# A planned attention-and-MLP kernel on one core: batch 0's query denominators in two groups, and its order searched anew

## The chip, the core and the metric

One Trainium2 chip, one of its cores. The time is the device time of one execution in microseconds; runs of one kernel are summed up by their median. Engines are named as in the profile: PE (TensorE), DVE (VectorE), ACT (ScalarE), POOL (GpSimd) and SP (SyncE, which here only issues transfers).

## What is computed

Linear attention with second-degree features, then an MLP on the result, float32 in and out:

```
# q, k, v: (4 batches, 4 heads, 1088 tokens, 32); S1, S2: (8, 32)
a = S1 @ x;  b = S2 @ x                          # per token and head, x is q or k
phi(x) = outer(a, b).reshape(64)
kv = sum over tokens of outer(phi(k), v)         # (64, 32) per batch and head
z  = sum over tokens of phi(k)
num = phi(q) @ kv
den = phi(q) @ z + 1e-6
x = num / den                                    # 4352 tokens, 128 wide (4 heads x 32)
h = x @ w_in                                     # 128 -> 2048
g = h if h >= 1 else 0 if h <= -1 else (h + 1)**2 / 4
out = g @ w_out                                  # 2048 -> 128
```

The weights and S come as float64 and are turned into float32 on the chip.

## The kernel before

**Work and tiles.** The MLP is cut into 9 chunks of 512 tokens (the last has 256) and 16 blocks of 128 hidden features: 144 units (`unit`, L824). A unit multiplies up (L838: three matmuls into a PSUM bank, since x and w_in are each held as a high and a low part), computes g (ACT Relu at L849 and Square at L851, DVE max and min at L854), splits g into a high and a low part (L860, L862 or L854 for the high part, L866 for the low part) and multiplies down into its chunk's sum (L880 twice, L885 once). `KINDS` says for each of the first 48 units which engine makes the high part: c on ACT, q on POOL, v on DVE; p makes the high part on ACT and the low part on DVE; w does not split g and multiplies down with one full float32 matmul (L890, which the trace shows as two records). The low part of c, q and v is made on POOL.

**Attention.** For each batch `keys` (L514) projects k (`abk`, L529), turns the result (`kab`, L535), forms the products phi(k) (`kp`, L553, on POOL where `KP_POOL` names the group, else on DVE) and sums kv (L589) and z (L560, then masked into `zm` at L568 and turned back at L573). `queries` (L616) does the rest. For batch 0 (the loop at L671) the 9 tiles of 128 tokens go in four groups of 2, 2, 3 and 2 tiles. For each group PE projects q (`abq`, L681), ACT copies the first factor out of PSUM (`as`, L689, with the second factor too where POOL is to multiply), DVE multiplies it with the projection on z (`terms`, L692), sums (`den`, L696), inverts (L698) and scales the first factor (`ap`, L701); DVE or, where `QP_POOL` names the group, POOL forms the products (`qp`, L707). PE turns the products (`tp`, L718), they are copied to `qt`, and PE multiplies them with kv (`nd`, L736); the result is split into `x_hi` and `x_lo` (L748). Chunk 0 needs groups 0 and 1, chunk 1 needs the others. The batches 1 to 3 use other code in `queries`, in groups of 3 tiles.

**Weights.** The eight pieces of w_in and w_out (`raw_i`, `raw_o`) are loaded and turned into float32 and into high and low parts (`from_double`, L416): an absolute value on ACT (L435), a clamp on POOL (L441), three integer steps on DVE (L444, L448, L452), the high part on ACT (L469), the low part on POOL, or on DVE where `IN_BANK` keeps the piece in PSUM (L471). Three raw buffers are shared by the eight pieces.

**Order.** Nothing is ordered by hand. Every step gets an engine, a cost and a due time (the constants at L22 to L62), and `Plan.run` (L147) lays the steps out on the five engines in a simulated order: at each moment an engine takes the ready step with the lowest due time for which buffers are free. The program is then issued in that order, so that each engine works through a fixed list and waits where an operand is late. Until the first units, PE's gaps are filled with idle matmuls (`warm`, L354). A down multiplication is due `AFTER` units after its up multiplication. [...]

Loads of batch 0 are split over the queues of SP and ACT; all others go through SP in the planned order.

Of the kernel before, what the change touches and what calls it, by code (L numbers as in the profile page):

```python
# [50 lines left out]
O0 = 0.8
KEYS = {1: (-39.7, -26.1), 2: (-27.9, -34.86), 3: (-37.22, -24.46)}
QEND = ((5.72, -6.14, -2.87), (7.51, 13.24, 4.11), (-9.22, -3.62, -6.11))
QLONG = (26.38, 22.3, 41.07)
FQ = ((-9.85, 4.5), (-11.89, 5.96), (-6.01, 0.82), (-7.59, 9.43))
FK = (-16.26, 9.99)
FKV = 6.85
WI = 5.68
WO = 2.37
# [270 lines left out]
def tile_kernel(ctx: ExitStack, tc: tile.TileContext, qT, kT, v, S, w_in, w_out, outT):  # L330
# [164 lines left out]
    QPART = [0, 0, 1, 1]  # L495
# [120 lines left out]
    def queries(b, kvb, dues):  # L616
# [3 lines left out]
        if not front:  # L620
# [29 lines left out]
            for gi, grp in enumerate(QGRP[b]):  # L650
                d = dues[gi]
                n = len(grp)
                g = slice(grp[0] * H, (grp[-1] + 1) * H)
                pool = (b, gi) in QP_POOL
                eng = nc.gpsimd if pool else nc.vector
                scaled = (lambda g=g: of(ap)[:, g]) if pool else (lambda g=g: kept()[:, g])
                tok = ap.part(gi) if pool else abq[0].part(("ap", gi))
                plan.add(d(0.3), "DVE", dve(n * HR), lambda scaled=scaled, g=g, n=n: nc.vector.tensor_tensor(
                    out=scaled(), in0=flat(0)[:, g], in1=rec()[:, g].broadcast_to([P, n * H, R]), op=ALU.mult),
                    r=[*both, abq[0].part("r")], w=[tok])  # L660
                qp = Buf("qp", f"qp{b}_{gi}", [P, 3, H * F])
# [6 lines left out]
                plan.add(d(0.5), "DVE", turned32(n * H * F), lambda qp=qp, grp=grp, n=n: nc.vector.transpose(  # L668
                    out=of(qt)[:, grp[0] : grp[-1] + 1].rearrange("p t f -> p (t f)"),
                    in_=of(qp)[:, :n].rearrange("p t f -> p (t f)")), r=[qp], w=[qt.part(gi)])  # L670
        for gi, grp in enumerate(QGRP[b] if front else ()):  # L671
# [4 lines left out]
            abc = bank(f"abq{b}_{gi}", tags[0])

            def project(abc=abc, grp=grp):
                for i, t in enumerate(grp):
                    for k, c in enumerate((slice(0, F), slice(F, 2 * F))):  # L680
                        nc.tensor.matmul(of(abc)[c, i * 96 : (i + 1) * 96], lhsT=of(qb)[:, t, c],  # L681
                                         rhs=proj[:, k:][:, :H, : 3 * R], start=True, stop=True)
# [4 lines left out]
            f = 2 if pool else 1
            a = Buf("as", f"as{b}_{gi}", [P, 2, 3 * H, R])
            plan.add(d(0.1), "ACT", act(m * R * f), lambda a=a, view=view, m=m, f=f: nc.scalar.copy(  # L689
                of(a)[:, :f, :m].rearrange("p f m i -> p m f i"), view()[:, :, :f]), r=[abc], w=[a])  # L690
            ti = (4 * b + gi) % 2
            plan.add(d(0.15), "DVE", dve(m * R), lambda a=a, view=view, m=m, ti=ti: nc.vector.tensor_tensor(  # L692
                out=terms[ti][:, :m, :R], in0=of(a)[:, 0, :m], in1=view()[:, :, 2], op=ALU.mult),
                r=[abc, a], w=[("terms", ti)])
            den = Buf("den", f"den{b}_{gi}", [P, 4 * H, 1])
            plan.add(d(0.2), "DVE", dve(m * 9), lambda den=den, m=m, ti=ti: nc.vector.tensor_reduce(  # L696
                out=of(den)[:, :m], in_=terms[ti][:, :m], axis=AX.X, op=ALU.add), r=[("terms", ti)], w=[den])
            plan.add(d(0.25), "DVE", 0.2, lambda den=den, m=m: nc.vector.reciprocal(  # L698
                out=of(den)[:, :m], in_=of(den)[:, :m]), r=[], w=[den])
            ap = Buf("ap", f"ap{b}_{gi}", [P, 3 * H, R])  # L700
            plan.add(d(0.3), "DVE", dve(m * R), lambda den=den, ap=ap, view=view, m=m: nc.vector.tensor_tensor(  # L701
                out=of(ap)[:, :m], in0=view()[:, :, 0], in1=of(den)[:, :m].broadcast_to([P, m, R]), op=ALU.mult),
                r=[abc, den], w=[ap])
# [309 lines left out]
```

## Time and profile before

| | |
|---|---|
| median of 3 runs | 228.28 us (228.09 to 228.99) |
| the profiled execution | 228.78 us |
| its span, first to last instruction | 226.8 us |
| PE busy in the span | 222.3 us (98%) |
| DVE busy | 207.4 us (91%) |
| ACT busy | 193.0 us (85%) |
| POOL busy | 191.7 us (85%) |
| granted TensorE clock | 1.000 of full speed in all slices |

The span is the distance from the first to the last instruction; the rest of the execution's time, 2.0 us, lies around it. Busy times are sums over an engine's instructions; a matmul's end is modelled, so consecutive matmuls overlap in the records and their pace is read from their starts. Engines work in the order of the program; what an instruction waited for is inferred from semaphores.

### The profile page before, as it was taken

The numbers are of one execution on the slowest core, as the hardware profiler recorded it, in microseconds if no ns is written. First come the engines' busy times: TensorE is split into PE (matmuls) and PEld (weight loads), VectorE is DVE, ScalarE is ACT, GpSimd is POOL, SyncE is SP. The second block draws the span as 40 slices with busy tenths as digits, with TensorE's granted clock in tenths as the row PEclk, the third lists the DMA queues.
The fourth block names the chain that finished last, engine by engine and source line by source line (L and its number), as shares of the span: only waits on it lengthen the run. The fifth ranks groups of instructions, "written<-read, shape, count | busy, mean of one in ns | idle before, by whom it ended". The sixth has DMA issues, their size and how long they took to land.

```text
span 226.8 us, 4962 instructions
## 1 busy us (share of the span) xinstructions
PE 222.3 (98%) x1737; PEld 171.3 (76%) x1739; DVE 207.4 (91%) x399; ACT 193.0 (85%) x385; POOL 191.7 (85%) x180
## 2 busy tenths in 40 slices
PE   8999999999999999999999999999999999999994
PEld 2568766778767788887576888888778888898894
DVE  3699989999988899899999999999968999998992
ACT  3279999999986989999586799898739999898993
POOL 5579799999995965999849699999966999999950
PEclk9999999999999999999999999999999999999999
DMA  6993450960001010001000100010000100100001
GB/s 176 411 349 131 135 197 10 353 253 0 0 3 46 8 46 1 0 0 46 3 3 0 49 1 0 1 48 3 0 0 0 49 0 1 46 4 0 0 0 69
DMA packets 4775, 13.86 MB, mean 61 GB/s; under 512 B 528, under 2 KB 912, under 8 KB 4752
## 3 DMA queue, kind: packets, MB, share of 16 engines
q1 hardware_dynamic: 4320, 12.91, 15.9%
q10 hardware_dynamic: 432, 0.66, 0.8%
q8 instruction: 13, 0.21, 0.4%
q14 instruction: 10, 0.08, 0.1%
HBM read 11.34 MB, written 2.23 MB: 60 GB/s over the span
## 4 chain that ended last, share of the span: by engine, by line
PE 95%; DMA 2%; DVE 1%; issue 0%; ACT 0%; POOL 0%; POOLq 0%
PE h L838 42%; PE acc L880 27%; PE acc L885 13%; PE acc L890 2%; DMA k<-in_kT 2%; PE nd L762 2%; PE kv L589 2%; PE abk L529 2%; PE warm L354 1%; PE tp L718 1%; PE abq L635 1%; PE nd L736 1%; PE z L573 1%; PE z L560 0%; PE kv L609 0%
## 5 line engine op out<-in xcount | busy, mean ns | idle before, releaser
L866 POOL TENSOR_TENSOR g_lo<-g,g_hi 128x512 fp32r<-128x512 f32 (+1 forms) x123 | 149.5, 1249 | 17.1 <-DVE g_hi L854 6.8
L849 ACT ACTIVATE s<-h 128x512 f32<-128x512 f32 (+1 forms) x144 | 80.7, 581 | 11.6 <-PE h L838 8.1
L851 ACT ACTIVATE s<-s 128x512 f32<-128x512 f32 (+1 forms) x144 | 86.5, 622 | 2.6
L854 DVE SCALAR_TENSOR_TENSOR g<-h,s 128x512 f32<-128x512 f32 (+1 forms) x123 | 79.7, 651 | 6.4 <-ACT s L851 4.9
L854 DVE SCALAR_TENSOR_TENSOR g_hi<-h,s 128x512 fp32r<-128x512 f32 (+1 forms) x97 | 62.1, 643 | 0.9 <-ACT s L851 0.6
L838 PE MATMUL h<-x_hi,wi_hi 128*128 128x512 f32 (+1 forms) x144 | 56.0, 389 | 0.0
L838 PE MATMUL h<-x_hi,wi_lo 128*128 128x512 f32 (+1 forms) x144 | 54.5, 378 | 0.0
L838 PE MATMUL h<-x_lo,wi_hi 128*128 128x512 f32 (+1 forms) x144 | 54.4, 378 | 0.0
L885 PE MATMUL acc<-g_lo,wo_hi 128*128 128x512 f32 (+1 forms) x138 | 52.8, 384 | 0.0
L880 PE MATMUL acc<-g_hi,wo_hi 128*128 128x512 f32 (+1 forms) x138 | 52.5, 381 | 0.0
L880 PE MATMUL acc<-g_hi,wo_lo 128*128 128x512 f32 (+1 forms) x138 | 52.1, 378 | 0.0
L838 PEld LDWEIGHTS h<-x_hi,wi_hi 128*128 128x128 f32 x144 | 27.1, 188 | 8.0 <-DVE g L854 1.0
L885 PEld LDWEIGHTS acc<-g_lo,wo_hi 128*128 128x128 f32 x138 | 25.9, 188 | 6.8 <-issue 1.2
L838 PEld LDWEIGHTS h<-x_hi,wi_lo 128*128 128x128 f32 x144 | 27.1, 188 | 5.2
L838 PEld LDWEIGHTS h<-x_lo,wi_hi 128*128 128x128 f32 x144 | 27.1, 188 | 4.9 <-issue 0.2
L880 PEld LDWEIGHTS acc<-g_hi,wo_hi 128*128 128x128 f32 x138 | 26.0, 188 | 5.9 <-issue 1.4
L880 PEld LDWEIGHTS acc<-g_hi,wo_lo 128*128 128x128 f32 x138 | 26.0, 188 | 4.6
L553 POOL TENSOR_TENSOR kp<-kab 128x768 f32<-128x768 f32 (+2 forms) x5 | 9.7, 1963 | 1.1 <-DVE kab L535 1.1
L663 POOL TENSOR_TENSOR qp<-ap,qab 128x768 f32<-128x768 f32 x7 | 10.7, 1522 | 0.0
L860 ACT CAST g_hi<-g 128x512 fp32r<-128x512 f32 x16 | 10.0, 633 | 0.6 <-DVE g L854 0.6
L866 DVE TENSOR_TENSOR g_lo<-h,g_hi 128x512 fp32r<-128x512 f32 (+1 forms) x15 | 8.7, 609 | 0.9 <-ACT g_hi L860 0.7
L354 PE MATMUL warm<-const-bfloat16-1.0 128*128 128x512 bf16 x24 | 8.3, 474 | 1.2 <-PEq L1001 0.8
(108 smaller groups left out, 195.6 us busy)
## 6 DMA issues: line engine op xcount, KB each, us to landing
raw_i<-in_w_in SPq DMA_DIRECT2D x4, 512.0 KB, 4.9
raw_o<-in_w_out SPq DMA_DIRECT2D x4, 512.0 KB, 5.2
outT<-o SPq DMA_DIRECT2D x8, 256.0 KB, 2.1
k<-in_kT SPq DMA_DIRECT2D x3, 576.0 KB, 7.7
q<-in_qT SPq DMA_DIRECT2D x3, 576.0 KB, 6.1
v<-in_v SPq DMA_DIRECT2D x3, 576.0 KB, 6.2
k<-in_kT SPq DMA_DIRECT2D x1, 448.0 KB, 4.7
v<-in_v SPq DMA_DIRECT2D x1, 320.0 KB, 6.7
```

What stands on the lines that cost most here:

```text
L354: plan = Plan(rings, lambda n: nc.tensor.matmul(of(warm)[:, :n], lhsT=ones[:, :P], rhs=ones[:, :n], start=True, stop=True), WARM)
L529: nc.tensor.matmul(of(abs_[k])[c, : NTL * D].rearrange("p (t f) -> p t f", f=D), lhsT=s_pair[rows, k * D : (k + 1) * D], rhs=of(kb)[rows, ...
L553: eng.tensor_tensor(out=of(kp)[:, grp[0] : grp[-1] + 1].rearrange("p t (h i j) -> p (t h) i j", h=H, i=R), in0=x[0].unsqueeze(3).broadcast ...
L663: lambda qp=qp, n=n, g=g, eng=eng, scaled=scaled: eng.tensor_tensor(out=of(qp)[:, :n].rearrange("p t (h i j) -> p (t h) i j", h=H, i=R), i ...
L838: nc.tensor.matmul(t[:, cols], lhsT=w[:, fj], rhs=x[:, xs], start=first, stop=last)
L849: plan.add(u, "ACT", act(n2), lambda: nc.scalar.activation(of(s)[:, :n2], of(h)[:, :n2], AF.Relu, bias=0.5, scale=0.5), r=[h], w=[s])
L851: plan.add(u, "ACT", act(n2, False), lambda: nc.scalar.activation(of(s)[:, :n2], of(s)[:, :n2], AF.Square), w=[s])
L854: nc.vector.scalar_tensor_tensor(out=of(out)[:, :n2], in0=of(h)[:, :n2], scalar=1.0, in1=of(s)[:, :n2], op0=ALU.max, op1=ALU.min)
L860: plan.add(u, "ACT", act(n2, False), lambda: nc.scalar.copy(of(g_hi)[:, :n2], of(g)[:, :n2]), r=[g], w=[g_hi])
L866: plan.add(u, "DVE" if late else "POOL", dve(n2) if late else pool_t(n2), lambda: eng.tensor_tensor(out=of(g_lo)[:, :n2], in0=of(g)[:, :n2 ...
L880: nc.tensor.matmul(of(acc)[:, into], lhsT=w[:, fj], rhs=of(g_hi)[:, cols], start=first and i == 0 and w is wo_hi, stop=False)
L885: nc.tensor.matmul(of(acc)[:, into], lhsT=wo_hi[:, fj], rhs=of(g_lo)[:, cols], start=False, stop=last and i == m - 1)
```

## The change

Batch 0's first factors, denominators and scaled factors are made in two groups: one of 4 tiles (the former groups 0 and 1) and one of 5 tiles (2 and 3), each with one projection bank, one copy, one `terms`, `den`, reciprocal and `ap`. The products, turns and everything after them stay in four groups; where POOL multiplies, ACT copies that group's second factor apart. With it, all constants of the order are new, among them the engine that splits each of the first units, which pieces' low parts go to DVE, and which products go to POOL.

```diff
-FILL = -62.42
-KINDS = 'wqcqwcwqcwqcqwvcpcpcpvqqwcpqvvpcvcvqccpcvppcccpq'
+FILL = -20.67
+KINDS = 'wwqccqvpwcwpcqqpqccpvpvqcqwcpcvqqpqqqpvpqqqpccqc'
-IN_BANK = ('i2', 'i3', 'o3')
+IN_BANK = ('i0', 'i2', 'i3', 'o0', 'o2', 'o3')
-AFTER = 6.29
+AFTER = 5.4
-KP_POOL = ((0, 1), (0, 2), (1, 0), (1, 1), (2, 0))
+KP_POOL = ((0, 0), (0, 1), (0, 2), (1, 0), (1, 1), (2, 0), (3, 0))
-QP_POOL = ((0, 3), (1, 0), (1, 1), (1, 2), (2, 0), (2, 2), (3, 1), (3, 2))
+QP_POOL = ((0, 1), (0, 3), (1, 0), (1, 1), (1, 2), (2, 0), (2, 1), (3, 0), (3, 2))
...
+        for ci, pair in enumerate(((0, 1), (2, 3)) if front else ()):
+            d = dues[pair[0]]
+            tiles = [t for gi in pair for t in QGRP[b][gi]]
...
+            plan.add(d(0.0), "PE", n * ABQ, project, r=[qb.part(ci), "proj"], w=[abc]).kind(1, 8 * n)
...
+            plan.add(d(0.1), "ACT", act(m * R), lambda a=a, view=view, m=m: nc.scalar.copy(
+                of(a)[:, 0, :m], view()[:, :, 0]), r=[abc], w=[a])
...
         for gi, grp in enumerate(QGRP[b] if front else ()):
...
-            plan.add(d(0.0), "PE", n * ABQ, project, r=[qb.part(QPART[gi]), "proj"], w=[abc]).kind(1, 8 * n)
...
+            abc, view, a, ap, g = chains[gi]
             pool = (b, gi) in QP_POOL
...
+            if pool:
+                plan.add(d(0.2), "ACT", act(m * R), lambda a=a, view=view, g=g: nc.scalar.copy(
+                    of(a)[:, 1, g], view()[:, g, 1]), r=[abc], w=[a.part(gi)])
```

The names in the lists below carry the batch or group first: `abq_1` is the projection of group 1, `mi` and `mo` are a piece of w_in or w_out on its way, `mago` its absolute value, `hci` and `hco` its clamp. The line numbers of the changed kernel are those of before up to L491, then mostly one less in `keys` and eight more behind the query code.

First ACT, from the projection of batch 0's queries on. Before:

```order
L689 COPY as_1_230<-abq_1_219 128x64
L689 COPY as_0_240<-abq_0_225 128x64
L469 CAST wi_hi<-magi_170 128x512
L689 COPY as_3_258<-abq_3_232 128x8x2x8
L689 COPY as_2_278<-abq_2_243 128x96
L435 ACTIVATE mago_280<-raw_o_126 128x512
```

and changed:

```order
L469 CAST wi_hi<-mi_189 128x512
L435 ACTIVATE mago_231<-raw_o_126 128x512
L710 COPY as_0_248<-abq_0_220 128x64
L687 COPY as_0_248<-abq_0_220 128x128
L710 COPY as_1_268<-abq_1_235 128x64
L687 COPY as_1_268<-abq_1_235 128x160
```

The weight steps `wi_hi` and `mago` now stand ahead of the first `as`, and `mago` reads a transferred piece.

Then DVE, at the denominators. Before:

```order
L692 TENSOR_TENSOR terms_85<-as_1_230,abq_1_219 128x8x8
L696 TENSOR_REDUCE den_1_250<-terms_85 128x8
L692 TENSOR_TENSOR terms_83<-as_0_240,abq_0_225 128x8x8
L698 RECIPROCAL den_1_250<-den_1_250 128x8
L696 TENSOR_REDUCE den_0_256<-terms_83 128x8
L701 TENSOR_TENSOR ap_1_272<-abq_1_219,den_1_250 128x64
L698 RECIPROCAL den_0_256<-den_0_256 128x8
L707 TENSOR_TENSOR qp_1_282<-ap_1_272,abq_1_219 128x512
```

and changed:

```order
L471 TENSOR_TENSOR wi_lo<-mi_189,wi_hi 128x512
L689 TENSOR_TENSOR terms_83<-as_0_248,abq_0_220 128x16x8
L693 TENSOR_REDUCE den_0_266<-terms_83 128x16
L695 RECIPROCAL den_0_266<-den_0_266 128x16
L689 TENSOR_TENSOR terms_85<-as_1_268,abq_1_235 128x20x8
L698 TENSOR_TENSOR ap_0_291<-abq_0_220,den_0_266 128x128
L693 TENSOR_REDUCE den_1_293<-terms_85 128x20
L715 TENSOR_TENSOR qp_0_298<-ap_0_291,abq_0_220 128x512
```

One chain serves groups 0 and 1; group 1's products are on POOL, and `wi_lo` of the first piece has come to DVE, ahead of the chain.

Last PE, around the first unit (`h` is a unit's up multiplication). Before:

```order
L560 MATMUL z_383<-kab_350 32x32 x9
L718 MATMUL tp_3_0_397<-ident,qp_3_348 128x128 x2
L718 MATMUL tp_2_0_404<-ident,qp_2_367 128x128 x3
L718 MATMUL tp_2_1_411<-ident,qp_2_367 128x128 x3
L718 MATMUL tp_3_1_418<-ident,qp_3_348 128x128 x2
L838 MATMUL h_421<-x_hi,wi_hi 128x512
L838 MATMUL h_421<-x_lo,wi_hi 128x512
L838 MATMUL h_421<-x_hi,wi_lo 128x512
L736 MATMUL nd_2_0_430<-qt_315,kvb_343 32x192
```

and changed:

```order
L726 MATMUL tp_2_1_379<-ident,qp_2_330 128x128 x3
L528 MATMUL abk_0_386<-k_229,s_pair 32x288 x4
L528 MATMUL abk_1_391<-k_229,s_pair 32x288 x4
L744 MATMUL nd_3_0_400<-qt_321,kvb_316 32x128
...
L744 MATMUL nd_2_0_414<-qt_321,kvb_316 32x192
...
L846 MATMUL h_427<-x_hi,wi_hi 128x512
L846 MATMUL h_427<-x_lo,wi_hi 128x512
L846 MATMUL h_427<-x_hi,wi_lo 128x512
L846 MATMUL h_436<-x_hi,wi_hi 128x512
```

Batch 1's key projection `abk`, which came earlier before, and groups 3 and 2 of `nd` now stand ahead of the first unit; `z` of batch 1 comes behind the second.

## Rows read from the trace of the kernel before

**Rows 1.** The page: busy time, share of the span and instructions of each engine.

```profile
PE 222.3 (98%) x1737; PEld 171.3 (76%) x1739; DVE 207.4 (91%) x399; ACT 193.0 (85%) x385; POOL 191.7 (85%) x180
```

**Rows 2.** Busy time by stretch: us, then each engine's busy us and instructions, clock, DMA.

```profile
18.20:40.00 21.80, 21.77 (x215) 15.15 (x214) 20.79 (x43) 21.25 (x45) 19.99 (x20) 1.00 0.36 106
```

**Rows 3.** Timeline of PE, 10 to 22 us: start, us, line, records; idle before and releaser.

```profile
10.62 1.71 PE L681 MATMUL abq<-proj,q 128*64 128x96 f32 x36
...
14.20 0.83 PE L529 MATMUL abk<-k,s_pair 64*32 64x288 f32 x16
...
15.76 0.45 PE L736 MATMUL nd<-qt,kvb 64*32 64x128 f32 x16
...
16.84 0.38 PE L560 MATMUL z<-kab 128*32 128x32 f32 x18
17.15 1.31 PE L718 MATMUL tp<-ident,qp 128*128 128x128 f32 x10
18.22 0.48 PE L838 MATMUL h<-x_hi,wi_hi 128*128 128x512 f32 x1
...
18.77 0.40 PE L838 MATMUL h<-x_hi,wi_lo 128*128 128x512 f32 x1
19.09 0.77 PE L736 MATMUL nd<-qt,kvb 64*32 64x192 f32 x32
...
20.73 0.48 PE L838 MATMUL h<-x_hi,wi_hi 128*128 128x512 f32 x1
21.04 0.40 PE L838 MATMUL h<-x_lo,wi_hi 128*128 128x512 f32 x1
```

**Rows 4.** Timeline of PE around one unsplit unit's down multiplication, 35 to 37 us.

```profile
35.62 0.40 PE L838 MATMUL h<-x_hi,wi_lo 128*128 128x512 f32 x1
35.85 1.02 PE L890 MATMUL acc<-gd,o 128*128 128x512 f32 x2
36.63 0.49 PE L838 MATMUL h<-x_hi,wi_hi 128*128 128x512 f32 x1
36.97 0.40 PE L838 MATMUL h<-x_lo,wi_hi 128*128 128x512 f32 x1
```

**Rows 5.** Timeline of POOL, 8 to 21 us.

```profile
8.63 2.99 POOL L553 TENSOR_TENSOR kp<-kab 128x768 f32<-128x768 f32 x2
...
15.05 1.07 POOL L707 TENSOR_TENSOR qp<-ap,as 128x512 f32<-128x512 f32 x1 [0.83 <-PE abk L529]
...
16.66 4.33 POOL L553 TENSOR_TENSOR kp<-kab 128x1280 f32<-128x1280 f32 x2
```

**Rows 6.** Timeline of DVE, 8 to 18 us.

```profile
8.30 0.95 DVE L553 TENSOR_TENSOR kp<-kab,abk 128x768 f32<-128x768 f32 x1 [0.47 <-ACT abk L540]
...
10.72 0.69 DVE L452 SCALAR_TENSOR_TENSOR magi<-raw_i,mi 128x512 int32<-128x512 int32 x1
11.46 0.22 DVE L692 TENSOR_TENSOR terms<-as,abq 128x64 f32<-128x64 f32 x1
...
12.50 0.69 DVE L707 TENSOR_TENSOR qp<-ap,abq 128x512 f32<-128x512 f32 x1
...
17.30 0.49 DVE L748 TENSOR_TENSOR x_lo<-nd,x_hi 128x128 fp32r<-128x128 f32 x2 [0.20 <-ACT x_hi L488]
```

**Rows 7.** Timeline of ACT, 11 to 16 us.

```profile
11.22 0.54 ACT L689 COPY as<-abq 128x64 f32<-128x64 f32 x2 [0.77 <-PE abq L681]
...
14.46 0.70 ACT L435 ACTIVATE mago<-raw_o 128x512 f32<-128x512 f32 x1
15.04 0.29 ACT L488 COPY kvb<-kv 128x128 f32<-128x128 f32 x1
```

**Rows 8.** SP's issues by start, and transfers issued near 3.3 and 11.9 us: us to landing.

```profile
3.29 3.00 SPq L411 DMA_DIRECT2D raw_o<-in_w_out  x2
raw_o<-in_w_out SPq DMA_DIRECT2D x1, 512.0 KB, 8.1
q<-in_qT SPq DMA_DIRECT2D x1, 576.0 KB, 6.1
```

More of the change, by code (lines that the diff above doesn't have):

```diff
@@ L36 @@
 PAIR = False
-IN_BANK = ('i2', 'i3', 'o3')
-CAST = -47.26
-OW = (-2.77, 11.83, -26.31, 7.39)
+IN_BANK = ('i0', 'i2', 'i3', 'o0', 'o2', 'o3')
+CAST = -68.34
+OW = (11.62, 18.64, 38.06, -4.72)
 QB = 1
 TP = 0.109
-OWN = -1.75
-I0 = -8.89
-AFTER = 6.29
-AFTER_END = 8.5
-CAST_END = -145.24
-LATE = 6
-I1 = 2.05
-O1 = -2.11
-KP_POOL = ((0, 1), (0, 2), (1, 0), (1, 1), (2, 0))
[L51 to L59, printed above, removed]
-QP_POOL = ((0, 3), (1, 0), (1, 1), (1, 2), (2, 0), (2, 2), (3, 1), (3, 2))
-KVM = 0.46
-LOADS = {1: (-1.97, -0.59, 3.28), 2: (28.86, 16.82, 20.76), 3: (94.69, 106.52, 24.72)}
+OWN = -28.02
+I0 = -3.66
+AFTER = 5.4
+AFTER_END = 9.47
+CAST_END = -234.59
+LATE = 6
+I1 = -0.49
+O1 = 0.04
+KP_POOL = ((0, 0), (0, 1), (0, 2), (1, 0), (1, 1), (2, 0), (3, 0))
+O0 = -4.07
+KEYS = {1: (-38.51, -21.91), 2: (-30.12, -38.82), 3: (-37.66, -33.88)}
+QEND = ((0.65, -4.39, -1.2), (4.49, -9.06, 6.06), (0.56, -16.69, -3.75))
+QLONG = (20.48, 29.95, 36.37)
+FQ = ((-8.27, 2.66), (-13.24, 5.88), (-7.68, 7.27), (-11.84, 11.64))
+FK = (-8.87, 5.86)
+FKV = 5.3
+WI = 6.53
+WO = -1.47
+QP_POOL = ((0, 1), (0, 3), (1, 0), (1, 1), (1, 2), (2, 0), (2, 1), (3, 0), (3, 2))
+KVM = 0.62
+LOADS = {1: (-0.0, 3.23, 1.22), 2: (34.02, 27.19, 18.49), 3: (121.37, 98.47, 34.28)}
 def word_as_float(bits):
@@ L382, in tile_kernel @@
     for i in range(2):
-        t = cst.tile([P, 4 * H, R + 1], F32, name=f"terms{i}")
+        t = cst.tile([P, 5 * H, R + 1], F32, name=f"terms{i}")
         nc.gpsimd.memset(t, 1e-6)
@@ L494, in tile_kernel @@
     KCUT, VCUT = 7, 5
-    QPART = [0, 0, 1, 1]
     loaded = {}
@@ L670, in queries, with project @@
                     in_=of(qp)[:, :n].rearrange("p t f -> p (t f)")), r=[qp], w=[qt.part(gi)])
+        chains = []
+        for ci, pair in enumerate(((0, 1), (2, 3)) if front else ()):
+            d = dues[pair[0]]
+            tiles = [t for gi in pair for t in QGRP[b][gi]]
+            n = len(tiles)
+            m = n * H
+            abc = bank(f"abq{b}_{ci}")
+            def project(abc=abc, tiles=tiles):
+                for i, t in enumerate(tiles):
+                    for k, c in enumerate((slice(0, F), slice(F, 2 * F))):
+                        nc.tensor.matmul(of(abc)[c, i * 96 : (i + 1) * 96], lhsT=of(qb)[:, t, c],
+                                         rhs=proj[:, k:][:, :H, : 3 * R], start=True, stop=True)
+            plan.add(d(0.0), "PE", n * ABQ, project, r=[qb.part(ci), "proj"], w=[abc]).kind(1, 8 * n)
+            view = lambda abc=abc, m=m: of(abc)[:, : m * 24].rearrange("p (m c i) -> p m c i", c=3, i=R)
+            a = Buf("as", f"as{b}_{ci}", [P, 2, 5 * H, R])
+            plan.add(d(0.1), "ACT", act(m * R), lambda a=a, view=view, m=m: nc.scalar.copy(
+                of(a)[:, 0, :m], view()[:, :, 0]), r=[abc], w=[a])
+            plan.add(d(0.15), "DVE", dve(m * R), lambda a=a, view=view, m=m, ci=ci: nc.vector.tensor_tensor(
+                out=terms[ci][:, :m, :R], in0=of(a)[:, 0, :m], in1=view()[:, :, 2], op=ALU.mult),
+                r=[abc, a], w=[("terms", ci)])
+            den = Buf("den", f"den{b}_{ci}", [P, 5 * H, 1])
+            plan.add(d(0.2), "DVE", dve(m * 9), lambda den=den, m=m, ci=ci: nc.vector.tensor_reduce(
+                out=of(den)[:, :m], in_=terms[ci][:, :m], axis=AX.X, op=ALU.add), r=[("terms", ci)], w=[den])
+            plan.add(d(0.25), "DVE", 0.2, lambda den=den, m=m: nc.vector.reciprocal(
+                out=of(den)[:, :m], in_=of(den)[:, :m]), r=[], w=[den])
+            ap = Buf("ap", f"ap{b}_{ci}", [P, 5 * H, R])
+            plan.add(d(0.3), "DVE", dve(m * R), lambda den=den, ap=ap, view=view, m=m: nc.vector.tensor_tensor(
+                out=of(ap)[:, :m], in0=view()[:, :, 0], in1=of(den)[:, :m].broadcast_to([P, m, R]), op=ALU.mult),
+                r=[abc, den], w=[ap])
+            chains += [(abc, view, a, ap, slice(g0, g0 + len(QGRP[b][gi]) * H)) for gi, g0 in zip(pair, (0, len(QGRP[b][pair[0]]) * H))]
         for gi, grp in enumerate(QGRP[b] if front else ()):
@@ L675, in queries @@
             tags = ["h", "at"]
[L676 to L682, printed above, removed]
-            plan.add(d(0.0), "PE", n * ABQ, project, r=[qb.part(QPART[gi]), "proj"], w=[abc]).kind(1, 8 * n)
-            view = lambda abc=abc, m=m: of(abc)[:, : m * 24].rearrange("p (m c i) -> p m c i", c=3, i=R)
-            pool = (b, gi) in QP_POOL
[L687 to L703, printed above, removed]
+            abc, view, a, ap, g = chains[gi]
+            pool = (b, gi) in QP_POOL
+            if pool:
+                plan.add(d(0.2), "ACT", act(m * R), lambda a=a, view=view, g=g: nc.scalar.copy(
+                    of(a)[:, 1, g], view()[:, g, 1]), r=[abc], w=[a.part(gi)])
             qp = Buf("qp", f"qp{b}_{gi}", [P, 3, H * F])
```

8 lines of the change are left out of this document (4 added, 4 removed).

## The prediction

> **What bounds the kernel now.** I began with the page's busy times: PE is busy for 222.3 of 226.8 us [rows 1], which leaves nothing to gain from another engine unless it makes PE wait. Busy PE is not PE at its peak, so I read the pace from starts in the timeline. Two 512-wide matmuls of one unit start 0.23 us apart (35.62 to 35.85 [rows 4]), and from the first unit at 18.22 us to the last down multiplication PE departs from that pace hardly anywhere but where it changes between the units and something else: 0.32 us into `nd` (18.77 to 19.09) and 0.31 us for the first matmul of a unit after it (20.73 to 21.04) [rows 3]. That is 0.09 and 0.08 us too much, up to 0.11 after an unsplit unit (36.63 to 36.97 [rows 4]), so a foreign block between units costs about 0.2 us beside its own work. In the stretch by engine PE has 21.77 of 21.80 us behind the first unit, with ACT at 21.25, DVE at 20.79 and POOL at 19.99 [rows 2]: PE ends last, the others are close behind. So the time is the start of the first unit, plus PE's remaining work, plus waits that appear. I work out these three.
>
> **The start of the first unit.** I follow the changed order with the durations of before.
>
> *POOL and DVE to 11 us.* The third key group's products come to POOL: 3 x 1.5 us instead of 2 (2.99 for two, from 8.63 [rows 5]), so batch 0's `kp` ends at 13.14 and not 11.62. DVE loses its own 0.95 us [rows 6]; it starts on the first weight piece some 0.5 us earlier, and the last integer step, which started at 10.72 and took 0.69, ends near 10.9 instead of 11.4 [rows 6]. What does the longer `kp` cost? The last kv sums come near 13.9, the copies and the turn bring `kvb` at about 15.1, before its 15.33 of before (15.04 + 0.29 [rows 7]); it is not the last to come. Nothing, then.
>
> [...] On 768 elements POOL takes 1.5 us where DVE takes 0.95, 1.57 times as long [rows 5, 6]. [...]
>
> *ACT from 11 us.* The copies `as` began at 11.22 [rows 7]. Now `wi_hi` and `mago` stand ahead of them. `mago` reads a piece issued at 3.29 that lands 8.1 us later, at 11.4 [rows 8], and ACT's next instruction follows such a step by 0.58 us (14.46 to 15.04 [rows 7]). The copies start near 12.0 and the first pair is done near 12.4: queued behind that landing, they come 0.8 us later. The projection itself is no later than its 10.62 [rows 3] but for one idle matmul of 0.2 us, and DVE's `wi_lo` lies inside the wait.
>
> *The denominators.* The first `terms` started at 11.46 and the first products at 12.50, ending 13.19 [rows 6]: eight small steps in 1.04 us, 0.13 each, since the two groups' steps interleave. Two chains of 16 and 20 columns replace four of 8 or 12: eight steps fewer, each of the rest longer by 0.06 to 0.1 us. Starting at 12.45, `terms`, `den` and reciprocal depend on each other (0.3, 0.3 and 0.2 us with their hand-overs), the other group's `terms` and `den` lie between, and `ap` takes 0.28. Group 0's products end on DVE near 14.55, group 1's on POOL (1.07 us [rows 5], from about 13.8) at 14.9. Before, the first ended at 13.19.
>
> *PE from the first products to the first unit.* Turn, two copies of 0.33 each and `nd` follow. The first `nd` started at 15.76 before [rows 3], held by `kvb`; now it is held by `qt` and starts near 15.85, the second near 16.35. The last `x_lo` of chunk 0 ends at 17.76, against 17.30 + 0.49 = 17.79 before [rows 6]. So chunk 0 is ready at the same time. But PE goes through its list: turns of groups 2 and 3 (1.07 us, 17.15 to 18.22), `abk` of batch 1 (0.76, 14.20 to the 14.96 of the next turn; 0.7 without the change of kind) and `nd` of groups 3 and 2 (0.70, 19.09 to 19.79) [rows 3] now all stand between 16.8 and the first unit. It starts near **19.4 us**, 1.2 us later. `abk` needs batch 1's k, which SP now issues near 11.3 instead of 6.33, behind a piece that waits for a buffer; second in line it should land near 16.5, and by the slowest comparable row (q, 6.1 us after its issue [rows 8]) at 17.4, before 17.9. Bounds: 18.8 if `mago` does not hold the copies (0.6 us less, since then they wait for the projection alone), 20.0 if the landing or the chain is 0.6 us later.
>
> **PE's remaining work.** Counted from the first unit:
> - `nd` of groups 2 and 3 is done already: -0.70.
> - `z` of batch 1 is not: +0.31 (16.84 to 17.15 [rows 3]).
> - five unsplit units instead of six. One costs 35.85 to 36.63, 0.78, and the 0.11 of the change of kind: 0.89, against 3 x 0.23 for a split one [rows 4]: -0.2.
> - foreign blocks between units, unsplit ones aside: 12 instead of 14 in the two lists: -0.4.
>
> Together -1.0. With the +1.2 of the start, the sum is **+0.2 us**: 229.0 for the profiled execution's 228.78. That execution lies 0.5 above the median, so I forecast 228.28 + 0.2, about **228.5 us**.
>
> **Waits that may appear.** I take none, and name the cover. Over the first units DVE, ACT and POOL have 0.5 to 1.8 us free in 21.8 [rows 2]. ACT has three fewer high parts to make (22 where 25 were) and DVE one subtraction more and two clamps fewer; POOL has six more casts of the high part, two `kp` groups and one `qp` more, against two low parts of weights gone: about 6 us more over the whole kernel. Behind the first unit POOL does batch 1's `kp` (4.33 us [rows 5]), a weight part, a cast, a weight part and the first low part, about 9.5 us from 19.8, so its first low part is ready near 29 when PE asks for it near 30.3; the margin stays above 1 us as far as I followed it, to the 16th unit. The tail behind the last unit is the same sequence, with one half unit more between, so the output's end keeps its distance. That `AFTER` falls from 6.29 to 5.4 units takes 1.2 us (0.9 x 1.36) off each low part's time to be ready.
>
> **The rivals.**
>
> *Slower: POOL becomes late between 24 and 60 us.* It decides if batch 1's `kp` starts over 1.3 us later than 19.8, or if POOL's six extra microseconds fall before unit 30, where it has about 2 us free. For it: the shorter `AFTER`, ten casts turned to sixteen and every engine near full [rows 2]. Against it: my walk through the list finds each low part at least a microsecond early, and buffers for six units of low parts let POOL run behind. Price: PE stops for what POOL is short of, 1 to 2 us, so 229.5 to 230.5 us. Chance 0.19.
>
> *Faster: the early chain is shorter than I make it.* If `mago` does not hold the copies (the piece lands sooner), everything to the first unit moves up by as much as 0.6 us, and fewer changes of kind further on could give some tenths: start at 18.5, -0.7 in the sum, 227.6. Below that it would need the first unit at the 18.22 of before in spite of 1.4 us more work ahead of it, 227.3 or less. For it: eight idle matmuls stand behind batch 0's `z` and ahead of the first unit, where four stood, so PE has time to give. Against it: they stand between links of a chain that PE waits for. Chance 0.22, of which 0.06 over 0.5%.
>
> *Neither decides.* The fewer steps on DVE shorten nothing, since DVE waits for the copies. This is my forecast, +0.2; with its bounds, 18.8 to 20.0 for the start, it lies between 227.9 and 229.3 us. Chance 0.59.
>
> **How the numbers follow.** A measurement of this kernel can tell about 0.5%, 1.14 us, from no change: under 227.14 is faster, over 229.42 slower. The forecast's own range and most of the faster case lie within: 0.59 + 0.16, and a little of the slower case, 0.02. So 0.06 faster, 0.77 same, 0.17 slower. The range reaches into both rivals, 227.2 to 230.1 us.
>
> **What would show it.** Right: the first `as` copy near 12.0 behind `mago`, the first unit between 18.8 and 20.0 with `nd` of group 2 right before it, five unsplit units, and PE without a gap from there to the end. Wrong: the copies start near 11.3 (the landing was no wait); PE idle or slower than 0.23 us per matmul between 24 and 60 us, with POOL the releaser; `abk` of batch 1 waiting for its transfer; or the first unit after 20.

## The result, and the profile after

The changed kernel takes **231.43 us** (median of 4 runs, 230.90 to 232.38) against 228.63 (4 runs, 228.09 to 229.36) of the kernel before beside it: ratio 1.0138, 95% interval 1.0114 to 1.0161. That is slower by 2.8 us and outside the predicted range. The profiled execution took 232.38 us with a span of 229.4 us, at a granted clock of 1.00.

The page of the changed kernel, busy time by engine, against [rows 1]:

```profile
PE 224.7 (98%) x1742; PEld 172.5 (75%) x1744; DVE 204.4 (89%) x389; ACT 192.9 (84%) x381; POOL 197.6 (86%) x187
```

PE is still the busiest, and busier by 2.4 us, although from the first unit on it has less to do. First the part that I had walked through by hand. PE of the changed kernel, timeline (start, us, line, records):

```profile
10.45 1.71 PE L681 MATMUL abq<-proj,q 128*64 128x96 f32 x36
...
15.88 0.69 PE L744 MATMUL nd<-qt,kvb 64*32 64x128 f32 x32
16.50 1.51 PE L726 MATMUL tp<-ident,qp 128*128 128x128 f32 x10
17.95 0.71 PE L528 MATMUL abk<-k,s_pair 64*32 64x288 f32 x16
18.46 0.83 PE L744 MATMUL nd<-qt,kvb 64*32 64x128 f32 x32
19.21 0.50 PE L846 MATMUL h<-x_hi,wi_hi 128*128 128x512 f32 x1
...
20.80 0.38 PE L559 MATMUL z<-kab 128*32 128x32 f32 x18
```

ACT of the changed kernel:

```profile
11.18 0.70 ACT L435 ACTIVATE mago<-raw_o 128x512 f32<-128x512 f32 x1
11.79 0.19 ACT L710 COPY as<-abq 128x64 f32<-128x64 f32 x1
11.88 0.27 ACT L687 COPY as<-abq 128x128 f32<-128x128 f32 x1
```

POOL of the changed kernel:

```profile
8.23 4.46 POOL L552 TENSOR_TENSOR kp<-kab 128x768 f32<-128x768 f32 x3
...
19.98 4.32 POOL L552 TENSOR_TENSOR kp<-kab 128x1280 f32<-128x1280 f32 x2 [2.57 <-DVE kab L534]
...
27.30 3.79 POOL L874 TENSOR_TENSOR g_lo<-g,g_hi 128x512 fp32r<-128x512 f32 x3
```

This is the walk of the prediction: `mago` first and the copies 0.61 us behind it, three `kp` in 4.46 us, `abk` of batch 1 with no wait for its transfer, the first unit at 19.21 (19.4 was forecast), POOL's first low part started at 27.3 (ready at 28.6), and a single listed wait of PE behind the first unit, of 0.2 us. The loss is not there. It is in the long middle, where nothing was moved. Both kernels in the same 30 us, busy time by stretch (columns as in [rows 2]). The kernel before:

```profile
130.00:160.00 30.00, 30.00 (x135) 24.82 (x134) 30.00 (x53) 27.42 (x46) 28.91 (x23) 1.00 0.03 11
```

and the changed one:

```profile
130.00:160.00 30.00, 30.00 (x130) 24.20 (x130) 29.68 (x51) 26.77 (x44) 29.73 (x24) 1.00 0.03 10
```

PE is busy without a gap in both, at the same clock, and puts through 135 matmuls in one and 130 in the other. The timeline shows how. The kernel before:

```profile
145.48 0.39 PE L838 MATMUL h<-x_hi,wi_lo 128*128 128x512 f32 x1
145.71 0.39 PE L880 MATMUL acc<-g_hi,wo_hi 128*128 128x512 f32 x1
145.94 0.39 PE L880 MATMUL acc<-g_hi,wo_lo 128*128 128x512 f32 x1
146.16 0.39 PE L885 MATMUL acc<-g_lo,wo_hi 128*128 128x512 f32 x1
146.39 0.39 PE L838 MATMUL h<-x_hi,wi_hi 128*128 128x512 f32 x1
146.62 0.39 PE L838 MATMUL h<-x_lo,wi_hi 128*128 128x512 f32 x1
146.84 0.39 PE L838 MATMUL h<-x_hi,wi_lo 128*128 128x512 f32 x1
```

and the changed one:

```profile
145.66 0.39 PE L846 MATMUL h<-x_hi,wi_lo 128*128 128x512 f32 x1
145.89 0.40 PE L888 MATMUL acc<-g_hi,wo_hi 128*128 128x512 f32 x1
146.13 0.40 PE L888 MATMUL acc<-g_hi,wo_lo 128*128 128x512 f32 x1
146.36 0.39 PE L893 MATMUL acc<-g_lo,wo_hi 128*128 128x512 f32 x1
146.59 0.40 PE L846 MATMUL h<-x_hi,wi_hi 128*128 128x512 f32 x1
146.82 0.39 PE L846 MATMUL h<-x_lo,wi_hi 128*128 128x512 f32 x1
147.06 0.40 PE L846 MATMUL h<-x_hi,wi_lo 128*128 128x512 f32 x1
```

The same six matmuls of one unit, 145.48 to 146.84 and 145.66 to 147.06: 1.36 against 1.40 us. No row has idle time or a releaser; a matmul starts 233 ns after the one before instead of 227. Below, **pace** is the mean distance between the starts of consecutive 512-wide matmuls from 60 to 220 us (some 560 distances, those of 0.20 to 0.26 us): 0.2276 before, 0.2323 in the change.

### The profile page after: what moved, and what is told of

The parts are those of the page before. It is cut to its first block, busy times and chain, and to the rows that moved or that the text cites. A ratio compares the mean times of both kernels' runs of the same rounds, so it can differ in the third digit from the quotient of the medians.

```text
span 229.4 us, 4959 instructions
## 1 busy us (share of the span) xinstructions
PE 224.7 (98%) x1742; PEld 172.5 (75%) x1744; DVE 204.4 (89%) x389; ACT 192.9 (84%) x381; POOL 197.6 (86%) x187
## 4 chain that ended last, share of the span: by engine, by line
PE 97%; DVE 1%; issue 0%; ACT 0%
PE h L846 42%; PE acc L888 27%; PE acc L893 13%; PE warm L354 4%; PE nd L770 2%; PE acc L898 2%; PE kv L588 2%; PE abk L528 1%; PE abq L634 1%; PE tp L726 1%; PE abq L681 1%; DVE x_lo L783 1%; PE z L572 1%; PE nd L744 1%; PE z L559 0%; DVE x_hi L489 0%
## 5 line engine op out<-in xcount | busy, mean ns | idle before, releaser
L862 DVE SCALAR_TENSOR_TENSOR g_hi<-h,s 128x512 fp32r<-128x512 f32 (+1 forms) x95 | 61.0, 644 | 1.3 <-ACT s L859 1.1
L846 PE MATMUL h<-x_hi,wi_hi 128*128 128x512 f32 (+1 forms) x144 | 57.2, 398 | 0.0
L888 PE MATMUL acc<-g_hi,wo_hi 128*128 128x512 f32 (+1 forms) x139 | 54.0, 388 | 0.0
L888 PE MATMUL acc<-g_hi,wo_lo 128*128 128x512 f32 (+1 forms) x139 | 53.1, 382 | 0.0
L552 POOL TENSOR_TENSOR kp<-kab 128x768 f32<-128x768 f32 (+2 forms) x7 | 13.6, 1967 | 2.6 <-DVE kab L534 2.6
L870 POOL CAST g_hi<-g 128x512 fp32r<-128x512 f32 x16 | 9.8, 619 | 3.6 <-DVE g L862 3.5
L354 PE MATMUL warm<-const-bfloat16-1.0 128*128 128x512 bf16 x28 | 9.5, 467 | 1.2 <-PEq L1009 0.8
L862 DVE SCALAR_TENSOR_TENSOR h<-h,s 128x512 f32<-128x512 f32 (+1 forms) x16 | 9.9, 623 | 0.0
```

The lines of the kernel that those rows point to most:

```text
L354: plan = Plan(rings, lambda n: nc.tensor.matmul(of(warm)[:, :n], lhsT=ones[:, :P], rhs=ones[:, :n], start=True, stop=True), WARM)
L552: eng.tensor_tensor(out=of(kp)[:, grp[0] : grp[-1] + 1].rearrange("p t (h i j) -> p (t h) i j", h=H, i=R), in0=x[0].unsqueeze(3).broadcast ...
L846: nc.tensor.matmul(t[:, cols], lhsT=w[:, fj], rhs=x[:, xs], start=first, stop=last)
L862: nc.vector.scalar_tensor_tensor(out=of(out)[:, :n2], in0=of(h)[:, :n2], scalar=1.0, in1=of(s)[:, :n2], op0=ALU.max, op1=ALU.min)
L870: plan.add(u, "POOL", pool_1(n2), lambda: nc.gpsimd.tensor_copy(of(g_hi)[:, :n2], of(g)[:, :n2]), r=[g], w=[g_hi])
L888: nc.tensor.matmul(of(acc)[:, into], lhsT=w[:, fj], rhs=of(g_hi)[:, cols], start=first and i == 0 and w is wo_hi, stop=False)
```

## The experiments

What has the change to do with the pace of matmuls that it doesn't touch? It enlarged tiles. A `terms` tile took 4 x 4 x 9 floats, 576 bytes of each partition, and takes 720 now. In the built programs every tile starts at a multiple of 32 bytes, the second `terms` stands 736 bytes behind the first instead of 576, and every tile behind the two 2 x (736 - 576) = 320 bytes further (`wi_hi` at 20032 instead of 19712). `as`, `den` and `ap` of batch 0, which lie ahead of the parts of g, grew as well. Theory A was that the weights and x had left a grid of 128 bytes. Its rivals: the pace comes from what the new order runs beside PE (B), or from a state of the chip in those runs (C).

**All tiles on multiples of 128 bytes**, in the changed kernel:

```diff
-        t = cst.tile([P, 5 * H, R + 1], F32, name=f"terms{i}")
+        t = cst.tile([P, 192], F32, name=f"terms{i}")[:, : 5 * H * (R + 1)].rearrange("p (m i) -> p m i", i=R + 1)
-            den = Buf("den", f"den{b}_{ci}", [P, 5 * H, 1])
+            den = Buf("den", f"den{b}_{ci}", [P, 32, 1])
```

> The changed kernel with the two terms tiles padded from 720 to 768 bytes per partition and the two small den tiles to 128, so that every later tile starts at a multiple of 128 bytes; the order is untouched. Theory A (addresses: the weights and x stand 64 bytes off a multiple of 128 since the change, and this slows every matmul): consecutive 512-wide matmuls of the body start 0.227 us apart again instead of 0.232, the last matmul some 4 us earlier, 226.5 to 227.5 us, ratio to the kernel before 0.990 to 0.997. Theory B (the new order sets the pace by what runs beside PE): spacing 0.232 and 231.4 us, ratio 1.014. Theory C (a state of the chip in those runs): no link with the edit, 228 to 231 us and the kernel before as variable.

Measured 231.51 us, ratio 1.0109 (1.005 to 1.0169), pace 0.2317. **The kernel before with the larger tiles:**

```diff
-        t = cst.tile([P, 4 * H, R + 1], F32, name=f"terms{i}")
+        t = cst.tile([P, 5 * H, R + 1], F32, name=f"terms{i}")
```

> The kernel before with its two terms tiles allocated as large as in the change (720 bytes per partition instead of 576) and nothing else: every tile behind them, weights, x and the parts of g alike, now starts 64 bytes off a multiple of 128. Theory A: spacing 0.232 to 0.233 us instead of 0.227, 232 to 234 us, ratio 1.015 to 1.025. Theories B and C: 228.3 us, ratio within 0.3% of 1.

Measured 228.26 us, ratio 0.999 (0.9961 to 1.0018), pace 0.2276. Theory A is wrong twice: on the grid the changed kernel stays slow, off it the kernel before stays fast. Two more of the changed kernel, with 64-byte gaps, one with a gap behind the weights (and one behind x, so that g comes to stand on the grid):

```diff
+    cst.tile([P, 16], F32, name="gap0")
     x_hi = cst.tile([P, NT + 128], F32R, name="x_hi")
     x_lo = cst.tile([P, NT + 128], F32R, name="x_lo")
+    cst.tile([P, 16], F32, name="gap1")
```

> The changed kernel with a 64-byte gap between the weights and x: the weights stay 64 bytes off a multiple of 128 as in the change, x and the parts of g stand on it. If the weights' address (what PE loads) sets the pace: 231 us and 0.232 us between matmuls, both up and down. If x's address (what PE streams) does: the down matmuls gain nothing, the up matmuls fall to 0.227, 228.5 to 229.5 us if half the loss is theirs. Theory B: 231.4 us.

and one ahead of them and one behind:

```diff
+    cst.tile([P, 16], F32, name="gap0")
     wi_hi = cst.tile([P, DFF], F32R, name="wi_hi")
...
+    cst.tile([P, 16], F32, name="gap1")
     x_hi = cst.tile([P, NT + 128], F32R, name="x_hi")
```

> The changed kernel with a 64-byte gap ahead of the weights and one behind them: the weights stand on a multiple of 128 bytes, x alone stays 64 bytes off, the parts of g stand on it. If the weights' address sets the pace: 0.227 us everywhere and 226.5 to 227.5 us. If x's does: up matmuls at 0.235, down at 0.227, about 229 us. Theory B: 231.4 us.

Measured 230.23 us (ratio 1.008, 1.0043 to 1.0117, pace 0.2302) and 231.52 us (1.011, 1.0024 to 1.0196, pace 0.2326). Neither side of A explains these: the second is no faster than the change although its weights stand on the grid. But the first has another pace with the same order, so addresses do matter, which speaks against B too. The kernel before, run beside these four, stayed at 228.39 us (median of 19 runs), which speaks against C.

The distances, in order, gave the next theory. In the changed kernel they repeat every two units, to a nanosecond or two, from 140 to 160 us (231, 233, 235, 232, 233, 240, then 227, 231, 232, 236, 229, 234), while DVE's and POOL's work drifts against PE's (DVE's `g` starts 0.62 us behind the first matmul of the latest unit at 150.00 us and 0.01 at 153.58, POOL's `g_lo` 1.14 at 147.73 and 0.02 at 157.78); and where the up multiplications of several units follow each other they fall to 226 and 227 ns (170.37 to 172.64 us). This points to PE itself, and to something that is missing where only x is streamed. What distinguishes these? I listed where each operand of a matmul starts, by the built programs, modulo 256 bytes. In the kernel before, all are alike: weights, x and g at 0 (the tiles of weights and x are multiples of 256 bytes long, and the pieces of a tile that the units use lie multiples of 512 apart). In the kernel of the second experiment too (64). In the changed kernel weights and x are at 64, and g at 128, since `den`'s two tiles added another 64. **Theory D**: PE's stream slows if it differs, in this place, from what PE loads meanwhile. The edit that makes them alike again in the changed kernel touches two tiles that are in use for about a microsecond:

```diff
-            den = Buf("den", f"den{b}_{ci}", [P, 5 * H, 1])
+            den = Buf("den", f"den{b}_{ci}", [P, 20 * H, 1])
```

> The changed kernel with its two small den tiles enlarged from 80 to 320 bytes per partition, which only moves the tiles behind them: the parts of g now start at the same place within 512 bytes (64) as the weights and x, as all three did in the kernel before (256); in the change g stood at 128 and the others at 64. Theory D (unequal places of what PE streams and what it loads meanwhile, within 512 bytes, slow its stream): consecutive 512-wide matmuls 0.227 us apart as in the kernel before, last matmul near 222 to 223 us, 226.3 to 227.8 us, ratio 0.991 to 0.997. Theory B (the new order sets the pace by what the other engines do beside PE): 0.232 us, 231.4 us, ratio 1.010 to 1.014.

Measured **229.10 us**, ratio 1.003 (1.0008 to 1.0052), pace 0.2276. The pace is what theory D expected. The time is not, it lies above the 226.3 to 227.8 us, because another, smaller loss is left, which is split up below. The order is the changed kernel's, row for row. Its stretch of 30 us:

```profile
130.00:160.00 30.00, 30.00 (x134) 24.84 (x133) 29.97 (x52) 27.52 (x46) 29.80 (x24) 1.00 0.03 10
```

And the reverse, in the kernel before (`[P, 4 * H, 1]` to `[P, 5 * H, 1]` for `den`, 64 to 96 bytes each):

> The kernel before with its small den tiles of batch 0 enlarged from 64 to 80 bytes (96 with rounding), nothing else: the parts of g move 64 bytes against the weights and x within 512, the relation that the change has. Order and work are those of the kernel before. Theory D: spacing 0.230 to 0.233 us, 230.5 to 233 us, ratio 1.010 to 1.020. Theory B: 0.227 us, ratio within 0.3% of 1.

Measured 230.62 us, ratio 1.0117 (1.005 to 1.0185), pace 0.2324. Sixteen bytes more in each of the two tiles of denominators (32 with rounding, so that g moves by 64) cost the kernel before 2.3 us. With x alone moved (a gap of 64 bytes ahead of `x_hi`, one of 448 behind `x_lo`):

> The kernel before with a gap of 64 bytes ahead of x and one of 448 behind it: x alone stands 64 bytes off the place of weights and g within 512. Theory D: slower than before, spacing 0.230 to 0.233 us, and now runs of up matmuls are slowed as well, ratio 1.008 to 1.020. Theory B: ratio within 0.3% of 1.

Measured 230.35 us, ratio 1.0077 (1.0052 to 1.0101), pace 0.2323. With g 256 bytes away (`[P, 12 * H, 1]`, 192 bytes) in the changed kernel:

> The changed kernel with the den tiles enlarged to 192 bytes: the parts of g stand 256 bytes from the place of weights and x within 512 (in the change 64). Theory D with a grid of 512 bytes: slow, 0.230 to 0.233 us, 230 to 232 us. With a grid of 256 or 64 times a divisor of 256: 0.227 us and 226.3 to 227.8 us. Theory B: 0.232 us, 231.4 us.

Measured 229.81 us, ratio 1.0058 (1.0024 to 1.0092), pace 0.2275: the pace is whole again, so 256 bytes apart count as alike, while the 128 of the first experiment did not. The time is again above its expectation, and 0.7 us above that of the kernel with `den` of 320 bytes, which has the same order and pace. The profiled executions of the two agree (spans 227.57 and 227.67 us), and the runs here scatter from 228.97 to 232.62, so this difference is not explained. Which two collide? **The weights alone moved**, in the kernel before:

```diff
+    cst.tile([P, 16], F32, name="gap0")
     wi_hi = cst.tile([P, DFF], F32R, name="wi_hi")
...
+    cst.tile([P, 112], F32, name="gap1")
     x_hi = cst.tile([P, NT + 128], F32R, name="x_hi")
```

> The kernel before with a gap of 64 bytes ahead of the weights and one of 448 behind them: the weights alone stand 64 bytes off, x and the parts of g have one place, so that everything PE streams agrees and only what it loads meanwhile differs. Theory D1 (a stream collides with the load beside it): slow everywhere, also in runs of up matmuls alone, 0.229 to 0.233 us, ratio 1.007 to 1.015. Theory D2 (one stream collides with the next): 0.227 us, ratio within 0.3% of 1.

Measured 230.40 us, ratio 1.0083 (1.0053 to 1.0112), pace 0.2333. All that PE streams agrees here; only what it loads differs. A run of up multiplications alone in this kernel, PE and its loads (PEld):

```profile
70.42 0.39 PE L840 MATMUL h<-x_hi,wi_lo 128*128 128x512 f32 x1
70.43 0.19 PEld L840 LDWEIGHTS h<-x_hi,wi_hi 128*128 128x128 f32 x1
70.66 0.39 PE L840 MATMUL h<-x_hi,wi_hi 128*128 128x512 f32 x1
70.66 0.19 PEld L840 LDWEIGHTS h<-x_lo,wi_hi 128*128 128x128 f32 x1
70.89 0.39 PE L840 MATMUL h<-x_lo,wi_hi 128*128 128x512 f32 x1
...
71.12 0.39 PE L840 MATMUL h<-x_hi,wi_lo 128*128 128x512 f32 x1
```

and the same run in the kernel before:

```profile
70.27 0.39 PE L838 MATMUL h<-x_hi,wi_lo 128*128 128x512 f32 x1
70.50 0.39 PE L838 MATMUL h<-x_hi,wi_hi 128*128 128x512 f32 x1
70.72 0.39 PE L838 MATMUL h<-x_lo,wi_hi 128*128 128x512 f32 x1
70.95 0.39 PE L838 MATMUL h<-x_hi,wi_lo 128*128 128x512 f32 x1
```

Three matmuls from 70.42 to 71.12 here, 0.70 us, and from 70.27 to 70.95 there, 0.68. Each load here runs beside the matmul ahead of it: it starts with it (70.66) and lasts 0.19 of its 0.23 us. So a difference between what PE streams and what it loads is enough to slow it. That it is the load for the next matmul, and not the place of a matmul's own weights, is argued from this overlap: in each kernel of the table all weights have one place, so the places cannot tell the two apart. With x moved, this same run is slower as well (226, 229 and 232 ns in turn); with g moved, where x and the weights agree, it falls to 226 and 227 ns. That the order plays no part in it is settled by the table: in either kernel the same list of instructions runs at both paces.

| kernel | weights / x / g modulo 256 bytes | pace, us |
|---|---|---|
| before; larger `terms` | 0 / 0 / 0; 64 / 64 / 64 | 0.2276; 0.2276 |
| change, `den` of 320; of 192 bytes | 64 / 64 / 64 in both | 0.2276; 0.2275 |
| change | 64 / 64 / 128 | 0.2323 |
| change, multiples of 128 | 128 / 128 / 0 | 0.2317 |
| change, gap behind the weights | 64 / 128 / 0 | 0.2302 |
| change, gaps around the weights | 128 / 192 / 0 | 0.2326 |
| before, g moved; x moved | 0 / 0 / 64; 0 / 64 / 0 | 0.2324; 0.2323 |
| before, weights moved | 64 / 0 / 0 | 0.2333 |

How large the loss is does not follow from one fixed cost for each unequal pair. In the kernel before with x moved, a run of up multiplications alone, all unequal, takes 229 ns each; the whole body, where they alternate with down multiplications whose places agree, takes 232.3. With x and g both unequal (64 / 128 / 0) the pace is 0.2302, better than with either alone. What sets the size, and whether a change from one streamed place to another adds to it, stays open.

**What is left of the loss** with the places made alike is 0.7 us (0.3% of 228.35). The profiles split it: from [rows 3] and the row below, the first unit starts 1.29 us later, from there to the last matmul PE needs 204.50 us instead of 205.33, and from the last matmul's start to the end of the span it is 3.66 us instead of 3.23. The sum, +1.29 - 0.83 + 0.43 = +0.89 us, is the difference of the two spans. PE of this kernel (`den` of 320 bytes):

```profile
11.02 1.71 PE L681 MATMUL abq<-proj,q 128*64 128x96 f32 x36
...
19.51 0.50 PE L846 MATMUL h<-x_hi,wi_hi 128*128 128x512 f32 x1
...
224.01 0.28 PE L893 MATMUL acc<-g_lo,wo_hi 128*128 128x256 f32 x1
```

*The end.* Of the transfers from 224 us on (packets, MB, share), two are pieces of instructions in the changed kernel, and none in the kernel before:

```profile
q8 instruction: 1, 0.02, 0.8%
q14 instruction: 1, 0.01, 0.4%
```

POOL's program has 330 instructions instead of 315. POOL closes the kernel, with two steps that the trace calls DRAIN. Here they are (shortest, median and longest in ns, then the first and last start in us) in the kernel before and in the one with `den` of 320 bytes:

```profile
L1009 POOLq DRAIN  x2: 39/58/78, 226.3 to 226.5; - x2
L1017 POOLq DRAIN  x2: 34/130/225, 227.0 to 227.4; - x2
```

The first of the two follows POOL's last semaphore by 0.06 us in the kernel before and by 0.35 in the other, and takes 78 and 225 ns: together about the 0.43 us. So I lengthened POOL's program of the kernel before by as many instructions:

```diff
+    last = cst.tile([P, 128], F32, name="last")
...
     for s in order:
         s.ways[s.taken][5]()
+    for i in range(15):
+        nc.gpsimd.memset(last[:, i : i + 1], 0)
```

> The kernel before with 15 one-column memsets at the end of POOL's program, which then has as many instructions as in the change (330 instead of 315); they run while PE still works. Theory T (the tail of the change is longer because POOL's longer program fetches one more piece of instructions at the very end): from the start of the last matmul to the end of the span 3.65 us instead of 3.23, with a gap of about 0.3 us ahead of POOL's last drain, ratio 1.001 to 1.003. Rival (the tail has another cause): 3.23 us and ratio 1.000.

In its profile the end takes 3.73 us, with one such transfer in the view and the same late drain:

```profile
q14 instruction: 1, 0.01, 0.2%
L1012 POOLq DRAIN  x2: 39/123/207, 226.4 to 226.8; - x2
```

The time is 228.88 us, ratio 1.001 (0.9989 to 1.0031): the profile shows the longer end, the runs can't resolve it. Over all profiles the end takes 3.6 to 3.7 us where POOL has 330 or 331 instructions, and 3.2 where it has 315 or 318 (the latter with the two groups, in the last experiment). So the longer end comes with the longer program of POOL. That POOL waits for the fetch is not shown: by the traces' times these transfers start only behind the last instruction (229.48 and 231.72 us in the change, whose span ends at 229.43; 227.39 with the memsets, where it ends at 227.07), when the late drain is over. What holds POOL there stays open.

*The start.* Does `mago` hold the copies? The planner, told the landing that the trace shows, puts it behind them (`den` has 320 bytes here too):

```diff
-        weights([O0, O1, first_unit[c] - WO][min(c, 2)], w_out, c, wo_hi, wo_lo, "o", *((None, None) if c else (-26.0, 10.0)))
+        weights([O0, O1, first_unit[c] - WO][min(c, 2)], w_out, c, wo_hi, wo_lo, "o", *((None, None) if c else (-26.0, 11.4)))
```

> The changed kernel with the places of operands made equal (den tiles of 320 bytes), and its planner told that the first piece of w_out lands at 11.4 us (as the trace shows) instead of 10.0: mago then stands behind the four copies as on ACT, PE's order is the same to the 30th unit but for four idle matmuls. Theory M (mago, waiting for its piece, holds the copies): the first copy starts 0.5 to 0.6 us earlier against the first projection of keys, the first unit 0.4 to 0.6 us earlier, 228.4 to 228.8 us, ratio 1.000 to 1.002. Rival (the chain waits elsewhere, for kvb or POOL's products): the copy moves, the first unit doesn't, 229.1 us, ratio 1.003.

Measured 229.88 us, ratio 1.0045 (1.0025 to 1.0065): slower, not faster. ACT of this kernel:

```profile
11.79 0.21 ACT L710 COPY as<-abq 128x64 f32<-128x64 f32 x1 [0.42 <-PE abq L681]
...
12.91 0.68 ACT L435 ACTIVATE mago<-raw_o 128x512 f32<-128x512 f32 x1
...
16.04 0.28 ACT L488 COPY kvb<-kv 128x128 f32<-128x128 f32 x1
```

PE's projection of this kernel, and the copy in the kernel with `den` of 320 bytes:

```profile
10.86 1.71 PE L681 MATMUL abq<-proj,q 128*64 128x96 f32 x36
12.08 0.20 ACT L710 COPY as<-abq 128x64 f32<-128x64 f32 x1
```

The copy starts 0.3 us earlier than there, and now it is PE that it waits for: one projection holds four tiles, where a first one of two was enough before. But the projection itself starts 0.16 us earlier in this run (10.86; 11.02 there), so the distances from its start tell more. The copy comes 0.60 us behind it in the kernel before (10.62 to 11.22 [rows 3, 7]), 0.93 here, 1.06 with `den` of 320 bytes and 1.34 in the change. So the larger group costs 0.33 us, and `mago` 0.13 us on top of it in the one profile and 0.41 in the other. And the first unit comes at 20.12 instead of 19.51: the new order brings `kvb` 0.9 us later (16.04; 15.11 there), `nd` starts 0.28 us later (16.59; 16.31), and turns behind it wait 0.23 us for DVE's `x_lo`. Of the theory little is left: `mago` holds the copies by less than it said, and the queue behind them matters more.

*The two groups without the new search* (the changed code with all constants of before, `den` of 320 bytes):

> The changed code with the constants of the order of before, and den tiles of 320 bytes, so that weights, x and the parts of g have one place within 256 bytes: the two groups alone, without the new search. mago stands behind the copies there. If the two groups by themselves are worth little, as the prediction has it: 228.0 to 229.3 us, ratio 0.998 to 1.004, spacing 0.227 us. If the new constants are what costs the 0.75 us that is left of the loss: not above before, ratio 0.996 to 1.000. If the edit needs its new constants: over 229.5 us.

Measured 234.28 us, ratio 1.0247 (1.0203 to 1.0291), at a pace of 0.2276: the first unit starts at 18.82, the second only at 24.22, behind batch 1's attention. The edit needs constants of its own; what it would be worth with the best ones stays open. No version of the change that was tried beats the kernel before.

## Why the prediction was wrong

The step that failed is the one in **PE's remaining work** that was not argued at all: it counted matmuls at 0.23 us [rows 4], as if PE's pace were a constant of the kernel. It gave -1.0 us from the first unit on. Measured: +1.24 us (19.21 to 225.78, 206.57 us, against 205.33), of which 2.07 are the pace (0.2323 instead of 0.2276 us), since the same list with the places made alike needs 204.50. What the pace hangs on is a line that the excerpt of the diff leaves out: `den` of batch 0 goes from `[P, 4 * H, 1]` to `[P, 5 * H, 1]`, which moves g by 64 bytes against weights and x. The prediction never asked what a tile's size moves. (The larger `terms`, alone in the kernel before, cost nothing, since they move all three together.)

Point by point, with the pace taken out:
- **Start of the first unit**, +1.2 forecast: +1.29 with places alike (+0.99 in the change, whose first transfer landed 0.4 us sooner in that run). Right in size, but in part by luck. The copies were put 0.8 us later because of `mago` alone. In the kernel with `den` of 320 bytes they are 0.86 later, of which the projection's own start is 0.40, its four tiles 0.33 and `mago` 0.13; in the change `mago` is 0.41 of 0.57, and the earlier projection takes 0.17 off. So the lower bound, 0.6 us less without `mago`, was mis-sized: it is 0.1 to 0.4.
- **Three `kp` on POOL for nothing**: right. They took 1.49 us each, as [rows 5] had it, 1.57 times DVE's 0.95 [rows 6], and `kvb` was not the last to come.
- **Remaining work of PE**, -1.0: -0.83.
- **No wait behind the first unit**: right, but for 0.2 us; POOL's first low part was ready at 28.6, where 29 was allowed for. The slower rival, POOL late between 24 and 60 us, did not happen.
- **"The output's end keeps its distance"**: wrong by 0.43 us, which comes with POOL's longer program.

With these the sum is +0.89 in the profile and +0.7 (0.2 to 1.2) in the runs, where +0.2 was forecast and the forecast's own range reached to +1.0. The mechanism that decided was in none of the rivals. The text did name the sign, "PE slower than 0.23 us per matmul", but only with POOL as its cause and only between 24 and 60 us.

## What to carry to other kernels

A tile that changes its size moves every tile behind it: in the built programs here the larger `terms` moved weights and x by 320 bytes, and `den` moved g by 64 against them. In a kernel like this one, bound by consecutive 512-wide matmuls with a load each, compare where the loaded and the streamed operands start modulo 256 bytes, before and after, and pad small tiles until these agree: it is one number, and here it was worth 2.3 us of 231. When a kernel slows with no gap and no releaser in the trace, compare start-to-start distances of one instruction in a stretch that the change left alone.

## What the runs showed of the hardware that was not expected

A 512-wide float32 matmul follows the one before by 226.7 ns in the best case (226, 227, 227 in turn, all of 140 to 160 us in the kernel before), and by 233.3 ns with the weights moved, where the load beside it starts 64 bytes away modulo 256. Differences of 64 and 128 bytes cost (pace 0.2333 with the weights moved by 64, 0.2317 in the change with g 128 away), 0 and 256 don't (0.2276 and 0.2275); smaller steps than 64 were not tried. In the change the distances lie between 226 and 240 ns from 140 to 160 us and repeat every twelve. In the kernel before it takes some matmuls after other work until the best pace is back: seven distances from 127.24 us (316, 224, 231, 236, 228, 233 and 231 ns, then 226), ten from 165.67, three from 110.07.

Only part of the slower pace reaches the end. With g moved in the kernel before, the fourth output copy is 0.16 us later (127.72 against 127.56), the second to last 1.94 us (224.38 against 222.44): up to 127 us PE has waits in the kernel before, covered by the modelled ends and so not listed as idle, and the lost nanoseconds come out of them. The largest such place is a projection of keys, in the kernel before and then with g moved:

```profile
108.76 1.38 PE L529 MATMUL abk<-k,s_pair 64*32 64x288 f32 x16
109.53 0.72 PE L529 MATMUL abk<-k,s_pair 64*32 64x288 f32 x16
```

It comes 0.78 us later with g moved and takes 0.66 us less. Behind 127 us some 360 matmuls at about 5.0 ns each make the 1.8 us.
